# S4D convolution and spatial-shift mixer: the statistics of h for twelve token tiles move out of the convolution, two tiles of x are normalised on GpSimd, and the order of instructions is set anew

## The chip, the core and the metric

The kernel runs on one core of one Trainium2 chip. Its engines are TensorE (PE, matmuls; PEld is its loading of weights), VectorE (DVE), ScalarE (ACT), GpSimd (POOL) and SyncE (SP, which issues most transfers). Each engine works through its own instructions in their order and waits on semaphores for the others. The metric is the device time of one execution in microseconds; the median of several is given.

## What is computed

x is 2048 tokens by 512 channels. A layer norm of x goes through a long convolution whose kernel is made from complex poles (128 modes for each channel), with a skip term; x is added. The sum h is normalised and goes through a mixer: a layer, a shift of the tokens by one or two in four groups of channels, a second layer, then a two-layer MLP, with two further layer norms and residual sums.

```python
P = jnp.exp((A * dt[:, None])[:, :, None] * pos[None, None, :])
K = 2.0 * jnp.einsum("dn,dnl->dl", C, P).real
Kf = jnp.fft.rfft(K, L2)                      # L2 = 2 * 2048
Uf = jnp.fft.rfft(u_t, L2)
y = jnp.fft.irfft(Uf * Kf[None, :, :], L2)[:, :, :L]
...
h = x + _A_ref(_layernorm(x, axis=-1), ...)   # y + u * D_skip
h2 = h + _B_ref(_layernorm(h, axis=-1), B_w1, B_w2, B_w3, B_w4)
```

In `_B_ref`: `h = gelu(LN(x) @ w1)`, four channel groups shifted by +1, -1, +2 and -2 tokens, `x1 = x + hs @ w2`, `x1 + gelu(LN(x1) @ w3) @ w4`.

## The kernel before

`h` holds x, later h, as 128 partitions (tokens) by 16 token tiles j by 512 channels, for the whole run. The kernel has two phases.

**The convolution** (`conv_phase`, line 304) transforms tokens by a two-stage FFT of length 4096 written as matmuls. The channels go in four spans s of 128 (`WID`), each made of eight groups g of 16 channels (`CH`). For each group, `table(g)` (line 570) builds the powers of the poles: `phases` adds two integer parts on GpSimd into `pt`, ScalarE takes sine and cosine of `pt`, and products of `E` and `ec` give amplitudes, `amx` for one stage and `amp` for the other; products `cs<-pt,amx`, `cs<-pt,amp`, `sn<-pt,amp` are the tables. `taps` turns them into the convolution's kernel by matmuls, the first stage of its transform follows (`stage_a_taps`, where ScalarE copies banks of PSUM to `at`, or `stage_a_turn`, where VectorE transposes the bank and PE needs fewer matmuls). For the tokens, `stage_a_x` and `spectrum_x` do the same; the spectra of spans 3 and 2 (`FAR`) are made early and wait in DRAM.

Each span ends with eight steps e: `product(s, e)` (line 803) multiplies two spectra into `u`, on VectorE (`u<-xs,bank`, 128 x 1024) or on GpSimd; where the table `SHARE["sum" + s]` names e, two sums `u<-u` of 128 x 256 halve the matmuls of the following `stage_b_inv` (`u,ms`, 16 in place of 32). `stage_a_inv` and `last_a_inv` finish the inverse and add to h. While span 3 is finished, bn_stats over the 384 channels of the other spans runs on the sixteen tiles (line 1097); `finish(q)` adds the last 128 channels of tiles 4q to 4q+3 and aggregates, for q = 0 to 2 in the mixer.

**What sets the order.** `Plan` is a list scheduler: each node has an engine, an estimated cost, what it reads and writes, and may have a due time made from the table `NOM`. `SHARE` says for each kind of step which groups, for the even and the odd spans, run on which engine (`amy`: amp on GpSimd, the others on VectorE; `csy`, `sny`: cs and sn with amp on GpSimd; `sq`: squares of amx on ScalarE, the others by the wider 896-column VectorE form; `turn`, `hadd`, `mul0`, `sum0` ... as their names say). Where PE would be idle the plan puts matmuls on `ident` that produce nothing that is used. Every instruction is issued by one helper, so nearly all have the same line, 86.

**The mixer** (`mixer_phase`, line 1124) is written in program order. `norm1(q)` applies the norm to four tiles (`xl`), `turn1(q)` transposes them on PE (`transposed`, into banks `xt`) and `split` makes a high part on ScalarE (`xt30h`) and a low part on VectorE (`xt30l`); `layer1(q, f)` multiplies by w1 in three products (`PROD`). The link from the convolution:

```python
norm1(3), finish(0), turn1(3), gelus(), root([0]), norm1(0), finish(1)
layer1(3, 0), layer1(3, 1), finish(2), layer1(3, 2), turn1(0), root([1, 2]), layer1(3, 3), norm1(1), raw3(0), raw4(0)
```

`some(13)` (lines 1527 and 1534) issues thirteen queued steps of the second norm at a slice of layer 3.

Of the kernel before, what the change touches and what calls it, by code (L numbers as in the profile page):

```python
# [1586 lines left out]
```

## Time and profile before

| | us |
| --- | --- |
| median of 3 runs | 716.33 (716.03 to 716.98) |
| the profiled execution | 715.36 |
| its span in the trace | 713.5 |
| PE busy | 664.4, 93% of the span |
| VectorE busy | 539.1, 76% |
| ScalarE busy | 420.5, 59% |
| GpSimd busy | 378.9, 53% |

The span is what the trace covers of the profiled execution. The shares of busy time are averages over stages that differ: x is loaded up to about 28 us; tables, spectra and spans 0 to 2 follow to about 283; span 3's products and inverses (called the tail) run to about 306; the link to about 330; then the mixer. Rows of groups read: out<-in, partitions x elements, count | busy us, mean ns of one | idle time before them and what ended it. Rows of the chain and the timeline begin with the start and the duration in us; square brackets hold the engine's idle time before the row and what ended it.

### The profile page before, as it was taken

Reading aid. Unit: us, or ns where it says so; the run is one execution under the profiler, and the core shown is the slowest. Engines: PE = TensorE matmul, PEld = TensorE weight load, DVE = VectorE, ACT = ScalarE, POOL = GpSimd, SP = SyncE. Lnnn points to the kernel's source line nnn. Section 1 sums busy time; section 2 is a strip of 40 time slices with the busy share of each in tenths; the row PEclk is TensorE's granted clock in tenths of the full one; section 3 lists DMA queues with packets and bytes.
Section 4 is the critical chain, followed back from the end, with each engine's and each line's share of the span. In section 5 each row is a group of like instructions: output and inputs, shape, how many; then the busy total and the mean of one; then the engine's idle time right before and its main releaser. Section 6 shows DMA issues by size and latency. Waiting matters only on the chain.

```text
span 713.5 us, 17581 instructions
## 1 busy us (share of the span) xinstructions
PE 664.4 (93%) x7324; PEld 522.9 (73%) x7324; DVE 539.1 (76%) x931; ACT 420.5 (59%) x724; POOL 378.9 (53%) x371
## 2 busy tenths in 40 slices
PE   5893899799999898989999999999999999999997
PEld 5892566575575584848888877888888888888886
DVE  6999997999999999987464777945568955544544
ACT  7789679777797886237536345555535544444430
POOL 1785676859989995302445304655343655543310
PEclk9997899999999999999999999999999999999999
DMA  8830154211301123010011001211111252112014
GB/s 210 263 124 16 47 166 152 61 38 40 62 18 31 46 86 98 2 60 1 1 30 30 1 3 57 60 48 57 45 46 43 79 158 60 45 45 58 3 28 118
DMA packets 44915, 45.24 MB, mean 63 GB/s; under 512 B 4900, under 2 KB 31524, under 8 KB 44836
## 3 DMA queue, kind: packets, MB, share of 16 engines
q1 hardware_dynamic: 44068, 43.07, 21.3%
q10 hardware_dynamic: 768, 1.05, 0.6%
q8 instruction: 57, 0.93, 0.6%
q14 instruction: 22, 0.18, 0.1%
HBM read 35.72 MB, written 8.39 MB: 62 GB/s over the span
## 4 chain that ended last, share of the span: by engine, by line
PE 58%; DVE 17%; ACT 15%; issue 4%; DMA 3%; POOL 2%; SPq 1%; DVEq 0%; ACTq 0%; POOLq 0%
PE l L86 21%; PE acc L86 10%; PE bank L86 7%; ACT pt L86 7%; DVE u L86 5%; DMA h<-in_A_u_dram 3%; PE l3f L86 3%; PE l3a L86 3%; PE l3b L86 3%; PE l3e L86 3%; PE l3c L86 3%; PE l3d L86 2%; PE l3g L86 2%; DVE cs L86 2%; DVE sn L86 2%
## 5 line engine op out<-in xcount | busy, mean ns | idle before, releaser
L86 ACT ACTIVATE pt<-pt 128x1056 f32<-128x1056 int32 x64 | 70.0, 1094 | 9.7 <-DVE cs L86 7.1
L86 POOL TENSOR_TENSOR pt<-p,s 128x1024 int32<-128x1024 int32 x32 | 65.0, 2035 | 14.5 <-DVE sn L86 13.1
L86 PE MATMUL bank<-at,tbs 128*64 128x128 f32 (+1 forms) x768 | 63.5, 311 | 2.8 <-DVE u L86 1.1
L86 PEld LDWEIGHTS bank<-at,tbs 128*64 128x64 f32 x768 | 44.5, 134 | 18.2 <-DVE u L86 2.6
L86 PE MATMUL bank<-u,ms 64*128 64x128 f32 x768 | 51.8, 281 | 3.7 <-DVE u L86 1.8
L86 PEld LDWEIGHTS bank<-ident 128*128 128x128 f32 x396 | 48.8, 203 | 6.5 <-issue 1.9
L86 PE MATMUL bank<-ident 128*128 128x128 f32 x396 | 51.8, 291 | 1.1 <-ACT at L86 1.1
L86 PEld LDWEIGHTS bank<-u,ms 64*128 64x128 f32 x768 | 45.7, 187 | 9.4 <-DVE u L86 2.4
L86 PE MATMUL bank<-cs 128*32 128x64 f32 x1024 | 33.8, 227 | 16.5 <-DVE scratch L86 12.9
L86 ACT COPY at<-bank 128x512 f32<-128x512 f32 x48 | 30.1, 636 | 30.5 <-PE bank L86 30.4
L86 PEld LDWEIGHTS bank<-cs 128*32 128x32 f32 x1024 | 25.1, 113 | 29.7 <-issue 20.8
L86 DVE TENSOR_TENSOR cs<-pt,amx 128x512 f32<-128x512 f32 x64 | 41.2, 683 | 5.8 <-ACT pt L86 2.9
L86 POOL TENSOR_TENSOR cs0w<-raw,cs0w 128x512 fp32r<-128x512 f32 x7 | 9.1, 1296 | 67.5 <-ACT cs0w L86 58.8
L86 DVE TENSOR_TENSOR u<-u,l3f 128x512 f32<-128x512 f32 x14 | 9.6, 685 | 44.5 <-PE l3f L86 44.5
L86 DVE TENSOR_TENSOR h<-h,l 128x512 f32<-128x512 f32 x48 | 32.4, 686 | 13.4 <-PE l L86 13.3
L86 POOL TENSOR_TENSOR cs1w<-raw,cs1w 128x512 fp32r<-128x512 f32 x7 | 9.2, 1308 | 60.6 <-ACT cs1w L86 57.7
L86 ACT ACTIVATE pt<-pt,halfpi 128x1056 f32<-128x1056 f32 x32 | 38.1, 1190 | 0.5
L86 ACT ACTIVATE u<-u 128x512 f32<-128x512 f32 x56 | 35.4, 633 | 1.8
L86 PE MATMUL bank<-sn 128*32 128x64 f32 x1024 | 32.8, 225 | 1.5 <-DVE sn L86 1.5
L86 POOL TENSOR_TENSOR amp<-E,ec 128x512 f32<-128x512 f32 x28 | 31.0, 1112 | 4.6 <-DVE ec L86 4.2
L86 DVE STREAM_TRANSPOSE at<-bank 128x1024 f32<-128x1024 f32 (+1 forms) x32 | 30.0, 979 | 2.6 <-PE bank L86 2.6
L86 POOL TENSOR_TENSOR cs<-pt,amp 128x512 f32<-128x512 f32 x23 | 28.0, 1215 | 7.1 <-ACT pt L86 4.1
(1160 smaller groups left out, 2108.8 us busy)
## 6 DMA issues: line engine op xcount, KB each, us to landing
raw<-in_B_w_dram SPq DMA_DIRECT2D x28, 256.0 KB, 2.8
h<-in_A_u_dram SPq DMA_DIRECT2D x32, 128.0 KB, 4.3
h<-in_A_u_dram SPq DMA_DIRECT2D x16, 256.0 KB, 4.1
rawa<-in_B_w_dram SPq DMA_DIRECT2D x14, 256.0 KB, 2.9
rawb<-in_B_w_dram SPq DMA_DIRECT2D x14, 256.0 KB, 2.9
ms<-in_mm_dram SPq DMA_DIRECT2D x4, 768.0 KB, 11.6
out_dram<-h SPq DMA_DIRECT2D x48, 64.0 KB, 1.7
xs<-far SPq DMA_DIRECT2D x10, 256.0 KB, 2.9
```

Source lines behind the costliest of these rows:

```text
L86: ins = f(*args, **kw)
```

## The change

The statistics over 384 channels stay in the convolution for tiles 12 to 15 alone, each held back to one of the first four products of span 3 (`BS`). Tiles 0 to 11 get one bn_stats over all 512 channels in `finish`, in the mixer, in two halves placed apart in the link; `root([1, 2])` is split in two. `norm_x` takes a slightly shorter rsqrt and gives tiles 4 and 15 of x to GpSimd (`nrm`). `phases` becomes two nodes of 8 channels each over half the columns; the two sums of a product become two nodes. In the link, all banks of `transposed` are of the wide kind; for q = 3, tiles 12 and 13 are turned first, then c by c the other two, each c split at once; `layer1(3, 0)` takes products of high parts ahead of low ones. `some(13)` becomes `some(11)`. `SHARE` and `NOM` get new values, so the whole order of the convolution is set anew. By the counts of the two programs' instructions, VectorE gets 13 amp products (4 before), 19 amx products of 896 columns (14), 13 of 512 (18) and 24 transposes of a bank (16), and loses 12 of its 44 statistics, 5 of 16 cs and sn products with amp, 4 of 16 sums `u<-u`, 4 of 8 additions of h and one normalisation. GpSimd has 19 amp products (28), 28 sums (16), 53 cs and sn products (48), 64 half phases (32 whole). PE has 352 matmuls `u,ms` (384), 352 `fas`/`kt` ones (576) and 231 fillers (198).

```diff
@@ line 24 @@
-    'amy': [[0, 1, 3, 4, 5, 6, 7], [0, 1, 2, 3, 4, 5, 6]],
-    'turn': [[2, 4, 5, 7], [5]],
-    'sum3': [[0, 4, 5, 6, 7], [0, 2]],
+    'nrm': [[4], [7]],
+    'amy': [[0, 1, 3, 4, 5, 6, 7], [1, 2, 3, 6]],
+    'turn': [[1, 2, 3, 5, 6, 7], [0, 3, 4, 5, 6, 7]],
+    'sum3': [[0, 1, 3, 4, 5, 6, 7], [0, 1, 2, 7]],
...
+BS = (0, 1, 2, 3)
@@ line 584 before, 585 after @@
-        def phases():
-            n = 2 * CH
-            o, o8 = slice(g % PG * n, g % PG * n + n), slice(g % NT * n, g % NT * n + n)
+        def phases(i):
+            n = CH
+            o, o8 = (slice(k * 2 * n + i * n, k * 2 * n + i * n + n) for k in (g % PG, g % NT))
             gp.tensor_tensor(
-                pi.rearrange("p (d i) -> p d i", i=33)[:, :, 0:32].rearrange("p d (a b) -> p d a b", b=8),
+                pi.rearrange("p (d i) -> p d i", i=33)[:, i * n : i * n + n, 0:32].rearrange("p d (a b) -> p d a b", b=8),
                 p8[:, o, :].unsqueeze(2).to_broadcast([128, n, 4, 8]),
@@ line 600 before, 601 after @@
-        add("POOL", 1.91, phases, r=["p8", "s"] + (["p81", "s1"] if 0 < g < PG else []), w=[kp])
+        for i in range(2):
+            add("POOL", 0.99, lambda i=i: phases(i), r=["p8", "s"] + (["p81", "s1"] if 0 < g < PG else []), w=[kp])
         if g == 0:
@@ line 844 before, 846 after @@
             add("ACT", 0.22 + n * 0.51e-3, lambda: act.copy(tap, taps_()), w=[uk], frees=p)
-            add("POOL", 3.0, pooled, r=keys, w=[uk])
+            add("POOL", 3.0, pooled, r=keys, w=[uk, ("made", s, e)])
         else:
-            add("DVE", 0.07 + 2 * n * 1.06e-3, mult, r=keys, w=[uk], frees=p)
+            add("DVE", 0.07 + 2 * n * 1.06e-3, mult, r=keys, w=[uk, ("made", s, e)], frees=p)
         eng = "POOL" if e in SHARE[f"sum{s}"][1] else "DVE" if e in SHARE[f"sum{s}"][0] else None
...
-            def sums():
-                en.tensor_tensor(q[:, 0], q[:, 0], q[:, 3], ALU.subtract)
-                en.tensor_tensor(q[:, 1], q[:, 1], q[:, 2], ALU.add)
-            add(eng, 2 * dve(2 * w_) if eng == "DVE" else 1.3, sums, w=[uk], port=True)
+            c = dve(2 * w_) + 0.02 if eng == "DVE" else 0.65
+            add(eng, c, lambda: en.tensor_tensor(q[:, 0], q[:, 0], q[:, 3], ALU.subtract), w=[uk], port=True)
+            add(eng, c, lambda: en.tensor_tensor(q[:, 1], q[:, 1], q[:, 2], ALU.add), w=[uk], port=True)
@@ line 974 before, 974 after @@
-        rs, la, lb, nb = (bs[:, :, 1, i] for i in range(4))
+        rs, lb, nb = (bs[:, :, 1, i] for i in range(3))
         root = lambda: plan.view(first)[:, 0:16]
...
             lambda: v.tensor_scalar(root(), mv[:, :, 1], EPS, None, ALU.add),
-            lambda: v.tensor_scalar(la, mv[:, :, 1], EPS, None, ALU.add),
             lambda: v.tensor_scalar(root().bitcast(I32), root().bitcast(I32), 1, None, ALU.logical_shift_right),
...
             ops += [
-                lambda: v.tensor_tensor(lb, la, root(), ALU.mult),
+                lambda: v.scalar_tensor_tensor(lb, mv[:, :, 1], EPS, root(), ALU.add, ALU.mult),
                 lambda: v.scalar_tensor_tensor(lb, lb, -0.5, root(), ALU.mult, ALU.mult),
...
         for i, op in enumerate(ops):
-            n = add("DVE", 0.09, op, r=["mv"], w=["rs"], bank=i == 0, frees=first if i + 1 == len(ops) else None, port=i == 1)
+            n = add("DVE", 0.09, op, r=["mv"], w=["rs"], bank=i == 0, frees=first if i + 1 == len(ops) else None)
             first = n if i == 0 else first
...
         for j in R16:
-            if j < LND:
+            if j % 8 in SHARE["nrm"][j // 8]:
+                add("POOL", 1.2, lambda j=j: gp.tensor_scalar(
+                    h[:, j, :], h[:, j, :], mv[:, j, 0:1], rs[:, j : j + 1], ALU.subtract, ALU.mult),
+                    r=["mv", "rs"], w=[("x", j // 2, c) for c in R4])
+            elif j < LND:
                 add("DVE", 0.46, lambda j=j: v.tensor_scalar(
@@ line 1094 before, 1097 after @@
         else:
-            for j in R16:
+            for i, j in enumerate(range(12, 16)):
                 add("DVE", 0.48, lambda j=j: v.bn_stats(bs[:, j, 0, :], h[:, j, 0 : OFF[s]]),
-                    r=[("h", q, r) for q in range(s) for r in range(WID[q] // 32)], w=[("bs", j)],
+                    r=[("h", q, r) for q in range(s) for r in range(WID[q] // 32)] + [("made", s, BS[i])], w=[("bs", j)],
                     at=TS[s] + NOM["st"] + 2 * j)
...
-    def finish(q):
-        for j in range(4 * q, 4 * q + 4):
+    def finish(q, tiles=range(4)):
+        for j in (4 * q + i for i in tiles):
             if q < 3:
-                v.bn_stats(bs[:, j, 1, :], h[:, j, OFF[NS - 1] :])
-        for j in range(4 * q, 4 * q + 4):
-            v.bn_aggr(cst["mv"][:, j, :], bs[:, j].rearrange("p a b -> p (a b)"))
+                v.bn_stats(bs[:, j, 0, :], h[:, j, :])
+        for j in (4 * q + i for i in tiles):
+            v.bn_aggr(cst["mv"][:, j, :], bs[:, j, 0, :] if q < 3 else bs[:, j].rearrange("p a b -> p (a b)"))
@@ line 1177 before, 1181 after @@
-    def transposed(tiles, name, wide=True, cs=range(4)):
-        b = [wide_bank(c, f"{name}_{c}") if wide else bank(f"{name}_{c}") for c in cs]
-        turn = lambda i, c: nc.tensor.transpose(b[c][:, i * 128 : i * 128 + 128], tiles[i][:, c * 128 : c * 128 + 128], ident)
-        if wide:
-            return [[turn(i, c) for i in range(4)] and split(b[c], f"{name}{c}") for c in cs]
-        for i in range(4):
-            for c in cs:
+    def transposed(tiles, name, first=0):
+        b = [wide_bank(c, f"{name}_{c}") for c in range(4)]
+        def turn(i, c):
+            nc.tensor.transpose(b[c][:, i * 128 : i * 128 + 128], tiles[i][:, c * 128 : c * 128 + 128], ident)
+        for i in range(first):
+            for c in range(4):
                 turn(i, c)
-        return [split(b[c], f"{name}{c}") for c in cs]
+        res = []
+        for c in range(4):
+            for i in range(first, 4):
+                turn(i, c)
+            res.append(split(b[c], f"{name}{c}"))
+        return res
@@ line 1205 before, 1216 after @@
     def turn1(q):
-        XT[q] = transposed(XL.pop(q), f"xt{q}", q < 3)
+        XT[q] = transposed(XL.pop(q), f"xt{q}", 2 if q == 3 else 0)
...
         n = 0
-        for c in range(4):
-            for wi, xi in (PROD if q < 3 else PROD[::2] + PROD[1:2]):
-                nc.tensor.matmul(b, W1[f][wi][:, c * 128 : c * 128 + 128], XT[q][c][xi],
-                                 start=(n == 0), stop=(n == 11))
-                n += 1
+        seq = [(c, wi, xi) for c in range(4) for wi, xi in PROD]
+        if (q, f) == (3, 0):
+            seq.sort(key=lambda k: 2 * k[0] + 3 * k[2])
+        for c, wi, xi in seq:
+            nc.tensor.matmul(b, W1[f][wi][:, c * 128 : c * 128 + 128], XT[q][c][xi], start=(n == 0), stop=(n == 11))
+            n += 1
         H1[q, f] = gelu(b, f"h1_{q}_{f}")
@@ line 1381 before, 1394 after @@
     gelus = lambda: nc.scalar.activation(zero, zero, AF.Gelu_apprx_tanh)
-    norm1(3), finish(0), turn1(3), gelus(), root([0]), norm1(0), finish(1)
-    layer1(3, 0), layer1(3, 1), finish(2), layer1(3, 2), turn1(0), root([1, 2]), layer1(3, 3), norm1(1), raw3(0), raw4(0)
-    layer1(0, 0), layer1(0, 1), layer1(0, 2), turn1(1), layer1(0, 3), layer2(0), layer2(1)
+    early, late = range(2), range(2, 4)
+    norm1(3), finish(0, early), turn1(3), gelus(), finish(0, late), root([0]), norm1(0)
+    layer1(3, 0), layer1(3, 1), finish(1, early), layer1(3, 2), turn1(0), finish(1, late), root([1]), layer1(3, 3), norm1(1), raw3(0), raw4(0)
+    layer1(0, 0), layer1(0, 1), finish(2, early), layer1(0, 2), finish(2, late), layer1(0, 3), turn1(1), root([2]), layer2(0), layer2(1)
     norm1(2), sum3(), layer1(1, 0), layer1(1, 1), layer1(1, 2), turn1(2), layer1(1, 3), load3(0), raw3(1)
@@ line 1517 before, 1531 after @@
                 stats2(j)
-            todo.extend(norm2_ops(2)), some(13)
+            todo.extend(norm2_ops(2)), some(11)
         if s == 2:
...
                 stats2(j)
-            todo.extend(norm2_ops(3)), some(13)
+            todo.extend(norm2_ops(3)), some(11)
         if s == 3 or s == 4:
```

How it moves instructions, at three places (names end in a buffer's number).

VectorE in the tail (`u0` and `u1` are the two buffers of products, `bs` the statistics). Before, from ahead of the third product of span 3:

```order
L86 BN_STATS bs_65<-h_63 128x6 x4
L86 TENSOR_TENSOR u1_121<-scratch_103,bank2_83 128x1024
L86 BN_STATS bs_65<-h_63 128x6 x2
L86 TENSOR_TENSOR u0_120<-scratch_103,bank3_84 128x1024
L86 BN_STATS bs_65<-h_63 128x6 x4
L86 TENSOR_TENSOR u1_121<-scratch_103,bank2_83 128x1024
L86 TENSOR_TENSOR u1_121<-u1_121 128x256 x2
L86 TENSOR_TENSOR u0_120<-scratch_103,bank3_84 128x1024
L86 TENSOR_TENSOR u0_120<-u0_120 128x256 x2
L86 BN_STATS bs_65<-h_63 128x6
L86 TENSOR_TENSOR u1_121<-p8_108,bank2_83 128x1024
```

After, from behind the first product:

```order
L87 BN_STATS bs_65<-h_63 128x6
L87 TENSOR_TENSOR u1_121<-xs1_123,bank0_81 128x1024
L87 BN_STATS bs_65<-h_63 128x6
L87 TENSOR_TENSOR u0_120<-scratch_103,bank2_83 128x1024
L87 BN_STATS bs_65<-h_63 128x6
L87 TENSOR_TENSOR u1_121<-scratch_103,bank3_84 128x1024
L87 BN_STATS bs_65<-h_63 128x6
L87 TENSOR_TENSOR u1_121<-u1_121 128x256 x2
L87 TENSOR_TENSOR u0_120<-scratch_103,bank2_83 128x1024
L87 TENSOR_TENSOR u0_120<-u0_120 128x256 x2
L87 TENSOR_TENSOR u1_121<-scratch_103,bank3_84 128x1024
```

The groups of two and four statistics between the products are gone, and single ones stand behind each of the first four. The fourth product (the second into `u1` of those shown after) now has its two sums ahead of the fifth.

PE in the link, from the turn of tile 14 to the first bank of layer 1 (`xt3_c` are the banks of the turned tiles 12 to 15, `xt3ch` and `xt3cl` their high and low parts, `cs0w` and `cs1w` hold parts of the first weights). Before:

```order
L86 MATMUL xt3_0_4161<-ident_58,xl14_4149 128x128
L86 MATMUL xt3_1_4162<-ident_58,xl14_4149 128x128
L86 MATMUL xt3_2_4163<-ident_58,xl14_4149 128x128
L86 MATMUL xt3_3_4164<-ident_58,xl14_4149 128x128
L86 MATMUL xt3_0_4161<-ident_58,xl15_4151 128x128
L86 MATMUL xt3_1_4162<-ident_58,xl15_4151 128x128
L86 MATMUL xt3_2_4163<-ident_58,xl15_4151 128x128
L86 MATMUL xt3_3_4164<-ident_58,xl15_4151 128x128
L86 MATMUL l1_3_0_4226<-xt30h_4181,cs0w_3727 128x512 x2
L86 MATMUL l1_3_0_4226<-xt30l_4182,cs0w_3727 128x512
L86 MATMUL l1_3_0_4226<-xt31h_4185,cs0w_3727 128x512 x2
L86 MATMUL l1_3_0_4226<-xt31l_4186,cs0w_3727 128x512
```

After:

```order
L87 MATMUL xt3_0_3952<-ident_58,xl14_3944 128x128
L87 MATMUL xt3_0_3952<-ident_58,xl15_3946 128x128
L87 MATMUL xt3_1_3953<-ident_58,xl14_3944 128x128
L87 MATMUL xt3_1_3953<-ident_58,xl15_3946 128x128
L87 MATMUL xt3_2_3954<-ident_58,xl14_3944 128x128
L87 MATMUL xt3_2_3954<-ident_58,xl15_3946 128x128
L87 MATMUL xt3_3_3955<-ident_58,xl14_3944 128x128
L87 MATMUL xt3_3_3955<-ident_58,xl15_3946 128x128
L87 MATMUL l1_3_0_4013<-xt30h_3966,cs0w_3536 128x512 x2
L87 MATMUL l1_3_0_4013<-xt31h_3972,cs0w_3536 128x512 x2
L87 MATMUL l1_3_0_4013<-xt30l_3967,cs0w_3536 128x512
L87 MATMUL l1_3_0_4013<-xt32h_3978,cs0w_3536 128x512 x2
```

The last two tiles are turned c by c, and each low part is used one step later, behind the next c's high part.

GpSimd at the end of the tables, around the last phases (`pt<-p8,s8`). Before:

```order
L86 TENSOR_TENSOR pt_112<-p8_108,s8_109 128x32x32
L86 TENSOR_TENSOR cs1_115<-pt_112,amp0_118 128x512
L86 TENSOR_TENSOR sn1_117<-pt_112,amp0_118 128x512
L86 TENSOR_TENSOR u0_120<-u0_120 128x256 x2
L86 TENSOR_TENSOR pt_112<-p8_108,s8_109 128x32x32
L86 TENSOR_TENSOR amp0_118<-E1_105,ec_102 128x512
L86 TENSOR_TENSOR sn0_116<-pt_112,amp0_118 128x512
L86 TENSOR_TENSOR u0_120<-u0_120 128x256 x2
L86 TENSOR_TENSOR cs1_115<-pt_112,amp0_118 128x512
```

After:

```order
L87 TENSOR_TENSOR pt_112<-p8_108,s8_109 128x16x32 x2
L87 TENSOR_TENSOR u0_120<-u0_120 128x256 x2
L87 TENSOR_TENSOR cs1_115<-pt_112,amp0_118 128x512
L87 TENSOR_TENSOR sn1_117<-pt_112,amp0_118 128x512
L87 TENSOR_TENSOR u1_121<-u1_121 128x256
L87 TENSOR_TENSOR pt_112<-p8_108,s8_109 128x16x32
L87 TENSOR_TENSOR u1_121<-u1_121 128x256
L87 TENSOR_TENSOR pt_112<-p8_108,s8_109 128x16x32
L87 TENSOR_TENSOR sn0_116<-pt_112,amp0_118 128x512
```

Each phase is in two halves, and single sums of a product stand between them.

More of the change, by code (lines that the diff above doesn't have):

```diff
@@ L23 @@
 PG = 4
-SHARE = {'mul0': [[1, 4], [0]], 'mul2': [[], []], 'amy': [[0, 1, 3, 4, 5, 6, 7], [0, 1, 2, 3, 4, 5, 6]], 'csy': [[5, 7], [0, 1, 2, 3, 4, 5, 7]], 'sny': [[1, 2, 6, 7], [0, 1, 2, 4, 5, 6, 7]], 'sq': [[0, 1, 2, 3, 5, 7], [1, 2, 4, 6]], 'turn': [[2, 4, 5, 7], [5]], 'hadd': [[0, 2, 6], [2, 3, 4, 5]], 'sum0': [[1, 2, 4], [4]], 'sum1': [[2], [5, 6]], 'sum2': [[4, 6, 7], [2, 4, 6]], 'sum3': [[0, 4, 5, 6, 7], [0, 2]]}
+SHARE = {'nrm': [[4], [7]], 'mul0': [[], [7]], 'mul2': [[6], []], 'amy': [[0, 1, 3, 4, 5, 6, 7], [1, 2, 3, 6]], 'csy': [[1, 4, 5, 6, 7], [0, 1, 2, 3, 4, 5, 7]], 'sny': [[1, 2, 3, 5, 6, 7], [0, 1, 2, 4, 5, 6, 7]], 'sq': [[0, 1, 5, 7], [1, 4, 7]], 'turn': [[1, 2, 3, 5, 6, 7], [0, 3, 4, 5, 6, 7]], 'hadd': [[0, 1, 2, 4, 6], [0, 2, 3, 5]], 'sum0': [[1, 4, 5], [1, 3, 4, 6]], 'sum1': [[0, 1], [0, 1]], 'sum2': [[1, 3], [1, 4, 5, 6]], 'sum3': [[0, 1, 3, 4, 5, 6, 7], [0, 1, 2, 7]]}
 XS = 2
@@ L34 @@
 LOOK = 0.05
+BS = (0, 1, 2, 3)
 FILL0 = 8.0
 FILLC, FILLN = 0.3, 128
-NOM = {'t0': 5334.34, 'per': 269.07, 'ln': 726.1, 'kg0': -4330.77, 'kgs0': -265.35, 'kg': 1.37, 'kgs': 337.02, 'ak': 482.29, 'ax': -575.41, 'b': -3.66, 'ib': -188.65, 'y': 2171.48, 'ys': 152.77, 'tr': 2105.83, 'exp': 1024.14, 'wt': 5260.29, 'pr1': 2915.83, 'pr2': 5242.12, 'st': -122.8, 'xa': -796.93, 'xs': -1631.75}
+NOM = {'t0': 7043.75, 'per': -130.02, 'ln': 950.41, 'kg0': -4725.44, 'kgs0': 3.78, 'kg': -162.35, 'kgs': 340.97, 'ak': 3031.32, 'ax': -642.19, 'b': 80.14, 'ib': -31.03, 'y': 3997.86, 'ys': 390.75, 'tr': 2244.98, 'exp': 3135.42, 'wt': 8336.6, 'pr1': 3284.83, 'pr2': 6195.32, 'st': -1499.02, 'xa': 896.41, 'xs': -2350.92}
 TURN = 2.0 ** 32
```

## The prediction

> **What bounds the kernel.** I read the busy shares by stage first, then the chain of waits, then the groups of the stage that the change rewrites. The windows (microseconds from the span's start) show four regimes:
>
> ```profile
> core 0: us, PE busy (x) PEld busy (x) DVE busy (x) ACT busy (x) POOL busy (x), PEclk, DMA share, GB/s
> 28.00:275.00 247.00, 215.59 (x4871) 157.30 (x4870) 230.54 (x349) 198.19 (x342) 195.24 (x169) 0.96 0.26 78
> 283.40:305.70 22.30, 22.10 (x309) 18.37 (x310) 21.96 (x37) 6.68 (x11) 6.67 (x8) 1.00 0.05 14
> 305.00:420.00 115.00, 111.64 (x546) 88.81 (x546) 75.58 (x185) 57.67 (x102) 36.34 (x62) 1.00 0.06 19
> 420.00:713.50 293.50, 288.49 (x1276) 236.32 (x1274) 183.96 (x288) 132.01 (x221) 124.47 (x110) 1.00 0.21 58
> ```
>
> From 28 to 275 (the body: tables, spectra, three spans) DVE is busy 230.54 of 247, ahead of every other engine: DVE sets the body. From 283.4 to 305.7 (the tail: the last span's products and inverses) PE and DVE are both full. From 305 on (link and mixer) PE is, and DVE has room. The chain of waits, in order of time, names the same:
>
> ```profile
> 283.38 13.66 PE bank L86 x199
> ...
> 299.14 0.47 DVE bs L86
> ...
> 303.91 1.85 DVE bs L86 x4
> ```
>
> So the tail runs along PE, with a stray statistic of h (`bs`) of 0.47 on the path.
>
> **Body, DVE: +6.2 us by rows.** Groups of DVE in the body (out<-in, shape, count | busy us, mean ns | idle before):
>
> ```profile
> L86 DVE TENSOR_TENSOR u<-xs,bank 128x1024 f32<-128x1024 f32 x21 | 25.5, 1217 | 2.4 <-ACT xs L86 2.2
> L86 DVE TENSOR_TENSOR amx<-E,amx 128x896 f32<-128x896 f32 x14 | 15.3, 1089 | 2.5 <-ACT amx L86 2.2
> L86 DVE TENSOR_TENSOR amx<-E,amx 128x512 f32<-128x512 f32 x17 | 11.7, 691 | 0.4 <-ACT amx L86 0.4
> L86 DVE STREAM_TRANSPOSE at<-bank 128x512 f32<-128x512 f32 x12 | 7.8, 696 | 0.0
> L86 DVE TENSOR_TENSOR u<-u 128x256 f32<-128x256 f32 x8 | 7.6, 991 | 0.0
> L86 DVE TENSOR_TENSOR cs<-pt,amp 128x512 f32<-128x512 f32 x9 | 6.5, 718 | 0.0
> L86 DVE TENSOR_TENSOR amp<-E,ec 128x512 f32<-128x512 f32 x4 | 3.2, 795 | 0.0
> ```
>
> Counting the instructions of the two programs, DVE gains nine amp products (9 x 0.795 = 7.2), eight transposes of a bank (8 x 0.696 = 5.6), five amx products in the 896 form (5 x 1.089 = 5.4) and one product of a spectrum (1.2): 19.4. It loses five amx products in the 512 form (3.5), five table products with amp (5 x 0.718 = 3.6), two additions of h and one normalisation of x (3 x 0.7, by the rows of the same size), and four sums u<-u (4 x 0.991 = 4.0): 13.2. Net +6.2. Nothing covers this, since the stage is DVE's.
>
> What gives some back. First, DVE's own waits in the body (instruction, releaser: us, count, longest):
>
> ```profile
> DVE cs L86 <- ACT pt L86: 2.9, 2, 2.0
> DVE amx L86 <- ACT amx L86: 2.6, 5, 1.0
> DVE cs L86 <- ACT amx L86: 2.2, 3, 0.9
> ```
>
> ACT squares amx for 13 groups instead of 18 and copies eight banks fewer, which DVE now transposes. The waits on squares fall by 5/18 of 4.8 (1.3); of the 2.9 on a late pt I take 1.2: -2.5, with 0 and -7.7 as ends. Second, waits that DVE spends inside an instruction beside GpSimd. The same u<-u takes 0.422 in the tail, where GpSimd is nearly idle, and one DVE step took 2.04 us beside a phase product:
>
> ```profile
> L86 DVE TENSOR_TENSOR u<-u 128x256 f32<-128x256 f32 x8 | 3.0, 422 | 0.1
> 132.46 2.04 DVE L86 SCALAR_TENSOR_TENSOR scratch<-scratch 128x256 f32<-128x256 f32 x1
> 132.27 1.95 POOL L86 TENSOR_TENSOR pt<-p,s 128x1024 int32<-128x1024 int32 x1
> L86 DVE TENSOR_TENSOR amp<-E,ec x4: 680/702/1095, 32.4 to 270.6; 128x512 f32<-128x512 f32 x4
> ```
>
> The two ran together and ended together, 134.50 and 134.22. The eight sums lost 8 x (0.991 - 0.422) = 4.6 that way. With each phase product cut into two halves of half the length, I take half of that, -2.3; the ends are +4.6 (other steps are caught as often, in place of those removed) and -4.6. Body: 6.2 - 2.5 - 2.3 = +1.4, between about +11 and -6.
>
> Here a rule of the Trainium skill speaks against the change: "SBUF — State Buffer", section "Who interferes with whom", says that VectorE and GpSimd share one port pair as an exclusive lock, that a VectorE instruction with two SBUF inputs contends with a GpSimd one that reads SBUF, and that whoever issues second is blocked for the whole instruction. The row at 132.46 agrees. By that rule the nine amp products (E and ec both in SBUF) would each wait about half a GpSimd operation, 0.6, and the body would be about 5 dearer (an estimate by that page). The amp row (shortest, median, longest) has a median of 0.702 and a longest of 1.095, so three in four were hardly held up, and I do not add it.
>
> **Body, GpSimd: about +2 us, hidden.**
>
> ```profile
> L86 POOL TENSOR_TENSOR pt<-p,s 128x1024 int32<-128x1024 int32 x30 | 61.1, 2040 | 14.4 <-DVE sn L86 13.1 <-DVE bs L86 0.9
> L86 POOL TENSOR_TENSOR amp<-E,ec 128x512 f32<-128x512 f32 x28 | 31.0, 1112 | 4.6 <-DVE ec L86 4.2
> L86 POOL TENSOR_TENSOR cs<-pt,amp 128x512 f32<-128x512 f32 x23 | 28.0, 1215 | 7.1 <-ACT pt L86 4.1 <-PE bank L86 1.8 <-issue 1.2
> L86 POOL TENSOR_TENSOR u<-u 128x256 f32<-128x256 f32 x12 | 8.9, 766 | 3.4 <-DVE u L86 3.2
> ```
>
> Nine amp products leave (-10.0), five cs/sn come (+6.1), eight sums come in the body (+6.1), two u<-u,xs products go (-2.6 at 1.3 each). Two normalisations of x come: no GpSimd row has one; between 0.77 and 2.04 each, nearest the 512-wide rows, 1.2 each (+2.4). The 32 added starts of half phases lie within these. Net +2 on 195.24 of 247: covered by 50 us of slack; were it gone, the pt of the next group would be late and DVE's waits on pt grow.
>
> PE needs 215.59 of 247 there; its 32 fewer matmuls of u, and the fas,kt shift to the turned form, cost nothing, since DVE hides it. SP's queue has the same 213 issues, a few swapped.
>
> **Tail: -2.0 us.** DVE drops twelve of sixteen 384-wide statistics, all eight products are summed instead of six, and GpSimd sums the last one too:
>
> ```profile
> L86 DVE BATCH_NORM_STATS2 bs<-h 128x6 f32<-128x384 f32 x16 | 7.9, 548 | 0.0
> 286.65 2.06 PE L86 MATMUL bank<-u,ms 64*128 64x128 f32 x32
> 289.67 1.16 PE L86 MATMUL bank<-u,ms 64*128 64x128 f32 x16
> 293.27 1.43 POOL L86 TENSOR_TENSOR u<-u 128x256 f32<-128x256 f32 x2 [1.30 <-DVE u L86]
> ```
>
> Two inverses shrink from 32 to 16 matmuls (2 x 0.90 = -1.8), and statistics of 0.47 leave the path between products in two places (-0.9). The last product's pair of sums goes to GpSimd, 1.43 instead of 2 x 0.422 on DVE, and only the last inverse can follow it: +0.7 (rounded up for the hand-over). The same on products 0 to 2 lies beside the next product. The block of four statistics at 303.91 filled DVE's wait for the last inverse and gives nothing. One end is -8: all that DVE drops (12 x 0.548 = 6.6, two additions of h 1.4), as if DVE alone set it. The other is 0: the short inverses only let PE fill the time with idle matmuls. I take -2.0, since PE is at 22.10 of 22.30, so the relief of the chain counts and not DVE's total.
>
> **Link: -0.9 us.** The new order has transposes of the last tiles ready c by c, high products ahead of low ones, and no bank shared with the split:
>
> ```profile
> 316.05 1.94 PE L86 MATMUL xt<-ident,xl 128*128 128x128 f32 x16 [0.95 <-ACT h L86]
> 319.12 0.73 PE L86 MATMUL l<-xt30h,cs0w 128*128 128x512 f32 x2 [1.13 <-DVE xt30l L86]
> 323.06 1.52 ACT L86 ACTIVATE xl<-h,rn,rr 128x512 f32<-128x512 f32 x2 [1.73 <-DVE rn L86]
> 327.42 1.91 PE L86 MATMUL xt<-ident,xl 128*128 128x128 f32 x16
> L86 DVE BATCH_NORM_STATS2 bs<-h 128x6 f32<-128x128 f32 x12 | 2.6, 278 | 0.0
> L86 DVE BATCH_NORM_STATS2 bs<-h 128x6 f32<-128x512 f32 x16 | 10.5, 670 | 0.9 <-DMA h<-in_A_u_dram 0.9
> ```
>
> PE's 1.13 wait on the split xt30l falls by about half (-0.6); the first c is complete after 10 of 16 transposes rather than 13, 0.12 each (-0.3). DVE's statistics grow from 0.278 to 0.670 on twelve tiles (+4.7) and the split roots add eleven small steps (at most +4.6, at 0.422, the shortest DVE row shown): all behind PE, which has 111.64 of 115 while DVE has 75.58. What is queued behind them on DVE is rn for tiles 0 to 3, so xl starts later by 4 x 0.39 - 0.3 = 1.3: from 323.06 plus two activations to 327.42, where PE turns them, there are some 2.8 us, less the 0.9 that PE arrives earlier. That margin of 0.6 keeps it covered; without it, up to 1 us returns.
>
> **Mixer: -0.5 us.** Two fewer queued steps are issued ahead of a slice's gelus in two places:
>
> ```profile
> 441.01 1.52 ACT L86 ACTIVATE x<-x,qo,qr 128x512 f32<-128x512 f32 x2 [4.97 <-DVE qo L86]
> 445.10 0.50 PE L86 MATMUL l<-cs0w,h_001h 128*128 128x512 f32 x1 [0.53 <-DVE u L86]
> ```
>
> PE's 0.53 at 445.10 goes, since the two activations of 1.52 no longer precede the gelu it needs. Ends 0 and -1.
>
> **Sum.** +1.4 - 2.0 - 0.9 - 0.5 = -2.0 on the profiled execution's 715.36, so 713.4; that execution stands 0.97 below the runs' median of 716.33, so I forecast a median of 714.3. A measurement of this kernel can tell about 0.2% from no change, 1.4 us.
>
> **Rivals.** (1) No change that can be told: the body costs about as much as the other stages save, +3.4 against -3.4: 716.3. For it: DVE's work over body and tail together stays nearly equal (+6.2 against -8), so the order mostly moves it to where DVE is also the limit. (2) The tail gets 6 of the 8 that DVE drops, and the body recovers all 6.2 from the waits above: -7.4 with link and mixer, 708.9. For it: DVE is at 21.96 of 22.30 in the tail; against: so is PE. (3) Slower: DVE's extra work in the body is paid in full, because the steps held up beside GpSimd are now the amp products and transposes in place of the sums, and half phases catch DVE twice as often for half as long. Place: the body; price +6.2, against -2.0 and -1.4: +2.8, 719.1. From a body of +4.8 on, that is with less than 1.4 of the 6.2 recovered, the kernel is measurably slower. For it: the amp product of 1.095 and the scratch step of 2.04; against: the median of 0.702. The rule of the Trainium skill named above stands beside this rival.
>
> **Numbers.** Chances: forecast 0.42, (1) 0.16, (2) 0.18, (3) 0.24. Faster by over 0.2%: 0.34 of the forecast and all of (2), 0.52. Within 0.2%: 0.08 of the forecast and all of (1), 0.24. Slower: 0.24. The range takes in the rivals' times with half a microsecond beyond, 708.5 to 719.5, and leaves out the far ends of the body (+11, -6); the forecast's own is 712.0 to 716.0.
>
> **What would show it.** In the profile after: u<-u on DVE in the body nearer 0.6 than 0.99 (phases halved), amp on DVE near 0.70 over thirteen of them, the start of the tail's first product within 2 us of 283, the tail about 20 long, no statistic of h of 384 columns outside tiles 12 to 15, layer 1's first product waiting under 0.6, and xt of tiles 0 to 3 not waiting on ACT. I am wrong if the tail starts 4 us or more later, if amp on DVE averages over 1 us, or if PE waits on xl.

## The result and the profile after

| | before | after |
| --- | --- | --- |
| median, us | 716.65 (716.03 to 717.20, 6 runs) | 709.89 (709.72 to 712.03, 6 runs) |
| profiled execution, us | 715.36 | 709.74 |
| its span, us | 713.5 | 707.6 |

The ratio of the two means is 0.9914, with a 95% interval of 0.9899 to 0.9928: 6.2 us faster, between 5.2 and 7.2 (the medians lie 6.8 apart). The forecast was 714.3, 2.0 us faster, in a range from 708.5 to 719.5.

Where the time came from is read best from a few events that both kernels have (start in us, in the profiled executions):

| event | before | after | earlier by |
| --- | --- | --- | --- |
| first product of span 3 (VectorE), end of the body | 284.99 | 280.05 | 4.94 |
| first transpose of the last inverse, end of the tail | 305.68 | 300.69 | 4.99 |
| first product of layer 1, link | 319.12 | 313.16 | 5.96 |
| transposes for the second norm's first tiles | 376.58 | 371.28 | 5.30 |
| layer 3 behind the slice with the queued steps | 448.15 | 442.01 | 6.14 |
| last 24 matmuls | 703.83 | 697.62 | 6.21 |

Nearly all of it is the body, the stage for which the prediction added time. The tail gave nothing, the link 1.0 and the mixer 0.8, of which 0.7 were lost between.

The body in both kernels, from 28 us to the first product of span 3; first before, then after:

```profile
28.00:284.98 256.98, 223.99 (x5067) 160.85 (x5066) 239.88 (x361) 202.65 (x349) 201.53 (x173) 0.96 0.27 80
```

```profile
28.00:280.04 252.04, 231.12 (x4659) 162.68 (x4661) 237.31 (x365) 199.54 (x337) 214.05 (x209) 0.98 0.27 80
```

The columns are the stretch, its length, and the busy time of PE, PEld, VectorE, ScalarE and GpSimd, each with its instructions. VectorE is 239.88 busy, then 237.31, with four instructions more. So VectorE did the longer list of work in less busy time, and its idle time fell from 17.1 to 14.7 us. GpSimd got 12.5 us more work and carried it. The groups that changed, of before (this stage; rows that stand in the prediction are not shown again):

```profile
L86 DVE TENSOR_TENSOR scratch<-scratch 128x256 f32<-128x256 f32 x5 | 6.5, 1315 | 0.0
L86 DVE SCALAR_TENSOR_TENSOR scratch<-scratch 128x256 f32<-128x256 f32 x7 | 4.8, 690 | 0.1
L86 DVE TENSOR_SCALAR sh<-thp 128x256 int32<-128x256 int32 x6 | 4.1, 676 | 0.0
L86 DVE TENSOR_TENSOR sn<-pt,amp 128x512 f32<-128x512 f32 x7 | 4.9, 695 | 0.0
```

And of after:

```profile
L87 DVE TENSOR_TENSOR cs<-pt,amx 128x512 f32<-128x512 f32 x64 | 41.3, 682 | 3.2 <-ACT pt L87 2.1 <-ACT amx L87 0.6
L87 DVE TENSOR_TENSOR amp<-E,ec 128x512 f32<-128x512 f32 x13 | 11.2, 869 | 0.0
L87 DVE TENSOR_TENSOR cs<-pt,amp 128x512 f32<-128x512 f32 x6 | 6.3, 1052 | 0.0
L87 DVE TENSOR_TENSOR sn<-pt,amp 128x512 f32<-128x512 f32 x5 | 5.4, 1080 | 0.0
L87 DVE TENSOR_TENSOR scratch<-scratch 128x256 f32<-128x256 f32 x5 | 4.5, 929 | 0.0
L87 DVE SCALAR_TENSOR_TENSOR scratch<-scratch 128x256 f32<-128x256 f32 x7 | 2.8, 413 | 0.0
L87 DVE TENSOR_TENSOR u<-u 128x256 f32<-128x256 f32 x4 | 2.0, 511 | 0.0
L87 DVE TENSOR_SCALAR sh<-thp 128x256 int32<-128x256 int32 x6 | 1.7, 290 | 0.0
```

The same `scratch` and `sh` steps, small ones that prepare a group of channels, cost 15.4 us before and 9.0 after (6.5 + 4.8 + 4.1 against 4.5 + 2.8 + 1.7), and a sum `u<-u` 0.511 instead of 0.991. The products with amp are longer than before (1.052 and 1.080 against 0.718 and 0.695). So the time that VectorE spends held up inside its instructions has moved to other steps and shrunk, by more than the prediction allowed. Its sum can be estimated: group VectorE's instructions in the body by operation, names and shape, and add up what each takes above the shortest of its group in the profiles of four kernels. That gives 34.2 us before and 25.7 after; of two kernels that come below, `b_half` has 32.9 and `a_whole` 29.2.

### The profile page after: what moved, and what is told of

Its sections match the earlier page's. It is cut to its first block, busy times and chain, and to the rows that moved or that the text cites. A ratio compares the mean times of both kernels' runs of the same rounds, so it can differ in the third digit from the quotient of the medians.

```text
span 707.6 us, 16728 instructions
## 1 busy us (share of the span) xinstructions
PE 671.8 (95%) x6886; PEld 524.0 (74%) x6886; DVE 538.2 (76%) x933; ACT 415.6 (59%) x708; POOL 393.2 (56%) x411
## 3 DMA queue, kind: packets, MB, share of 16 engines
q10 hardware_dynamic: 768, 1.05, 0.7%
## 4 chain that ended last, share of the span: by engine, by line
PE 56%; DVE 22%; ACT 8%; POOL 5%; issue 4%; DMA 3%; SPq 1%; DVEq 0%; POOLq 0%; ACTq 0%
PE l L87 18%; PE acc L87 11%; PE bank L87 8%; ACT pt L87 4%; DVE u L87 4%; DVE at L87 3%; DVE cs L87 3%; PE l3c L87 3%; PE l3f L87 3%; PE l3e L87 3%; DVE sn L87 3%; PE l3a L87 3%; PE l3d L87 3%; PE l3b L87 3%; PE l3g L87 3%
## 5 line engine op out<-in xcount | busy, mean ns | idle before, releaser
L87 ACT ACTIVATE pt<-pt 128x1056 f32<-128x1056 int32 x64 | 69.8, 1091 | 14.6 <-POOL pt L87 7.2
L87 POOL TENSOR_TENSOR pt<-p,s 128x512 int32<-128x512 int32 x64 | 70.9, 1122 | 6.0 <-DVE sn L87 5.6
L87 PEld LDWEIGHTS bank<-ident 128*128 128x128 f32 x462 | 59.1, 208 | 7.1 <-issue 4.6
L87 PE MATMUL bank<-ident 128*128 128x128 f32 x462 | 63.9, 297 | 0.0
L87 PE MATMUL bank<-u,ms 64*128 64x128 f32 x704 | 48.2, 282 | 3.2 <-DVE u L87 2.2
L87 PEld LDWEIGHTS bank<-u,ms 64*128 64x128 f32 x704 | 42.2, 187 | 8.5 <-issue 2.2
L87 DVE TENSOR_TENSOR h<-h,l 128x512 f32<-128x512 f32 x48 | 32.6, 687 | 14.8 <-PE l L87 14.7
L87 ACT COPY at<-bank 128x512 f32<-128x512 f32 x40 | 25.0, 626 | 28.7 <-PE bank L87 28.7
L87 DVE STREAM_TRANSPOSE at<-bank 128x512 f32<-128x512 f32 (+1 forms) x40 | 35.4, 925 | 2.7 <-PE bank L87 2.7
L87 POOL TENSOR_TENSOR cs<-pt,amp 128x512 f32<-128x512 f32 x26 | 32.8, 1262 | 5.9 <-DVE amp L87 3.5
L87 POOL TENSOR_TENSOR sn<-pt,amp 128x512 f32<-128x512 f32 x27 | 33.4, 1238 | 2.1 <-ACT pt L87 1.2
```

What stands on the lines that cost most here:

```text
L87: ins = f(*args, **kw)
```

## The experiments

Each run is compared with runs of the kernel before on its own chip; the ratio is that of the two. A remark for reading the profiles: three kernels whose order of the body is that of the kernel after (this kernel, `a_sum7`, `a_sumVh`) had their first product of span 3 at 280.05, 279.11 and 277.64, and four with that of before (that kernel, `b_link`, `b_some11`, `b_tail8`) at 284.99, 283.91, 285.50 and 285.23. Two executions of one body so differ by up to 2.4 us. About 1.2 of this lies ahead of the body: VectorE's first `cs<-pt,amx` starts at 27.75, 26.50 and 26.54, and at 28.19, 27.39, 28.20 and 27.31. From that product on, the means are 252.0 and 257.1, so the body is 5.1 shorter by all seven profiles, and 4.5 by the two kernels' own.

**Halves and tables: is it the half phases, or the new order?** Four kernels. `b_half` is the kernel before with

```diff
         def phases():
-            n = 2 * CH
-            o, o8 = slice(g % PG * n, g % PG * n + n), slice(g % NT * n, g % NT * n + n)
+            n = CH
+            for i in range(2):
+                o, o8 = (slice(k * 2 * n + i * n, k * 2 * n + i * n + n) for k in (g % PG, g % NT))
...
```

> The kernel before with each phase product on GpSimd issued as two halves of eight channels, back to back at the same place; nothing else changes. In the kernel after, VectorE's small steps and products in the body lose some 12 us less beside GpSimd, and the body is 4.9 us shorter. Theory A (short holds: half phases hold VectorE up half as long): the body gets 3 to 5 us shorter, about 712.5 us, and scratch, sh and u<-u on VectorE get shorter, as in the kernel after. Theory B (it is the new order that keeps these steps away from GpSimd): no change, 716.2 to 717.4, since the order is that of before. Theory C (halves cost GpSimd more than they give, 0.1 us a phase by the two means, 2.04 and 2 x 1.12): 717.5 to 719.

Measured: 1.0001 (0.9989 to 1.0013) of the kernel before, no change.

`a_whole` is the kernel after with the first half's step issuing the whole phase, and the second's nothing:

```diff
         def phases(i):
+            if i:
+                return
+            n = 2 * CH
```

> The kernel after with each phase product whole, issued where the first half stood; the order is otherwise the same. Theory A: 3 to 5 us slower than the kernel after, 713 to 715. Theory B: within 0.8 us of it, 709.1 to 710.7. Theory C: somewhat faster than the kernel after, 708 to 709.5.

Measured: 0.9997 (0.9985 to 1.0009) of the kernel before, against 0.9914 with halves: 0.83% or 5.9 us of 716 slower than the kernel after, nearly all of the 6.2 that it had gained.

`b_tables` is the kernel before with the two lines `SHARE` and `NOM` of after, `a_oldtab` the reverse:

```diff
-SHARE = {...}    # one kernel's own
-NOM = {...}
+SHARE = {...}    # the other's
+NOM = {...}
```

> The kernel before with the shares and due times of the kernel after (without the two normalisations on GpSimd): whole phases, sixteen statistics in the conv, the old link. Theory A: little gain or a loss in the body, 715 to 719, since the shares add work to VectorE and the holds stay long. Theory B: most of the body's gain, 711 to 713. The old link and the thirteen steps keep 1.3 us of the difference in both.

> The kernel after with the shares and due times of the kernel before: half phases, statistics in the mixer, new link, eleven steps. Theory A: 710 to 712.5 (the halves' gain and 1.3 us of link and mixer; the tail keeps its two long inverses). Theory B: 714.5 to 716 (link and mixer alone).

Measured: 1.0186 (1.0170 to 1.0202) and 1.0179 (1.0157 to 1.0200), both slower than every theory had it.

None of the theories stands as it was put. Halves alone give nothing, the tables alone cost 13 us, the rest of the code without them 13 us as well; only the kernel with both gains. Most of the loss in the two crossed kernels is waiting on VectorE. From 28 to 290 us, ahead of the first product of span 3 in both, first `b_tables`, then `a_oldtab`:

```profile
28.00:290.00 262.00, 235.96 (x4670) 163.63 (x4669) 235.15 (x363) 195.58 (x331) 200.23 (x174) 0.97 0.25 76
28.00:290.00 262.00, 222.94 (x5044) 163.43 (x5053) 236.32 (x353) 201.68 (x348) 202.15 (x200) 0.96 0.24 74
```

VectorE is idle for 26.9 and 25.7 us, against 17.1 and 14.7 in the bodies of before and after. In `b_tables` the tail is longer too (26.96 instead of 20.69).

What the halves do in each order is seen on the steps that GpSimd can hold up. GpSimd and VectorE in `b_half`, body:

```profile
L86 POOL TENSOR_TENSOR pt<-p,s 128x512 int32<-128x512 int32 x60 | 69.3, 1179 | 7.8 <-DVE sn L86 5.3 <-ACT pt L86 1.0 <-DVE bs L86 0.6
L86 DVE TENSOR_TENSOR u<-u 128x256 f32<-128x256 f32 x8 | 6.1, 798 | 0.0
L86 DVE TENSOR_TENSOR scratch<-scratch 128x256 f32<-128x256 f32 x5 | 4.8, 978 | 0.0
28.00:285.59 257.59, 224.14 (x5073) 160.97 (x5071) 238.53 (x360) 203.53 (x350) 208.71 (x204) 0.97 0.27 78
```

VectorE's held-up steps did get shorter (its busy time fell from 239.88 to 238.53 in a body 0.6 longer), but a pair of halves costs GpSimd 2.31 (69.3 / 30) instead of 2.04, 8.2 us over the body, and VectorE waited 2.0 more for others: 19.1 us idle instead of 17.1. In `a_whole`, where only the length of the phase differs from the kernel after:

```profile
28.00:284.15 256.15, 228.85 (x4642) 160.60 (x4641) 241.54 (x366) 200.12 (x339) 207.35 (x179) 0.98 0.26 79
L87 DVE TENSOR_TENSOR cs<-pt,amp 128x512 f32<-128x512 f32 x6 | 7.7, 1288 | 0.0
L87 DVE TENSOR_TENSOR u<-u 128x256 f32<-128x256 f32 x4 | 3.1, 766 | 0.0
```

Here busy time is 4.2 above that of the kernel after (241.54 against 237.31) and idle time the same (14.6 against 14.7), and the body is 4.1 longer. In the new order the halves are worth their whole saving of held-up time; in the old one it turns into waits. By the sums of held-up time given above, the new order alone took 5.0 off (34.2 to 29.2), the halves another 3.5 (to 25.7). Whether an order found for whole phases would do as well stays open, since that was not tried.

**Nine amp products, in both orders.** In `b_amp` and `a_amp` the nine products go to the other engine, each at its place in the order that is kept. The two lists of `amy` stand for the first span (g below 8) and for the three others, not for even and odd spans, so the three entries that the second list loses are nine products:

```diff
-        add(e, c, lambda: outer(eng, amy, ...), ...)
+        real = gp if g % 8 in OTHER[g >= 8] else v    # OTHER: the list 'amy' of the other kernel
+        add(e, c, lambda: outer(real, amy, ...), ...)
```

> The kernel before with the nine amp products that the change takes from GpSimd issued on VectorE, each at its old place in the order. By the prediction's first line (rows: VectorE sets the body, 9 x 0.795): the body 7 us longer, 723 to 724. If an order leaves VectorE room beside such steps, or GpSimd's relief shortens its waits and holds as much as the nine cost: 715 to 718 on the same scale. If holds come on top (half a GpSimd operation each): 727 and more.

> The kernel after with the nine moved amp products back on GpSimd, each at its place in the new order. If VectorE's sum of work set the body, it would lose 9 x 0.87 = 7.8 us and the run be 4 to 8 us faster (in the old order the same nine cost 4.0 us on VectorE). If the new order lives on GpSimd being relieved, GpSimd (214 of 252 us busy, +10) is late with cs and sn and the run is 3 us or more slower than the kernel after. In between, 0 to 2 us either way: the engines balance.

Measured: `b_amp` 1.0058 (1.0044 to 1.0072), 4.2 us slower than before; `a_amp` 0.9974 (0.9965 to 0.9983), 0.60% or 4.3 us slower than the kernel after. The body windows of `b_amp` and of `a_amp`:

```profile
28.00:288.94 260.94, 224.04 (x5064) 160.76 (x5065) 245.66 (x370) 202.64 (x349) 193.10 (x164) 0.97 0.26 78
```

```profile
28.00:283.84 255.84, 229.83 (x4652) 160.19 (x4654) 233.15 (x354) 198.80 (x335) 220.69 (x218) 0.98 0.27 79
```

In the old order nine products add 5.8 to VectorE's busy time and 4.0 to the body, about half of the 7.2 that the rows give: the nine take 7.3 (0.811 each, the mean of all thirteen), the other steps together take 1.5 less, and idle time shrinks by 1.8. In the new order taking them off VectorE saves 4.2 of busy time and brings 8.0 of idle time (22.7 against 14.7). VectorE is the busiest engine there, and still its sum of work does not set the body: relieved, it waits for others. What grew most are its waits for the squares of `amx` on ScalarE (2.9 to 7.1 us) and for `xs` (0.6 to 2.5); why these came later was not followed.

**The normalisation of two tiles.** `a_nrmV` issues them on VectorE at the same place (`gp.tensor_scalar` becomes `v.tensor_scalar`).

> The kernel after with the two normalisations of x that GpSimd makes issued on VectorE at the same place of the order. GpSimd took 2.1 us for each and VectorE (1.1 us) and PE (1.3 us) waited for them once. If GpSimd's slowness there costs time: 0.5 to 1.5 us faster than the kernel after. If VectorE's time is what counts (two steps of 0.78): up to 1.5 us slower. If the place has slack: no change.

Measured: 0.9944 (0.9931 to 0.9958), 0.30% or 2.1 us slower than the kernel after, a difference known to about 1.4. On GpSimd (kernel after, body) each took 2.085, far above the 1.2 of the prediction:

```profile
L87 POOL TENSOR_SCALAR h<-h,mvh,bs 128x512 f32<-128x512 f32 x2 | 4.2, 2085 | 0.0
```

It is still the right engine: two steps off VectorE are worth about 2 us, 1.6 of it their own 0.794 each.

**Link, statistics and the mixer alone.** `b_link` is the kernel before with the statistics of tiles 0 to 11 in the mixer and the new link, so with the hunks on `finish`, `transposed`, `layer1` and the three lines of the link; `b_some11` has `some(11)` alone.

> The kernel before with the statistics of h for tiles 0 to 11 made in the mixer alone and with the new link (transposes, order of layer 1's first bank, roots apart); shares, due times and the order of the conv up to the tail are those of before. By the steps of the prediction: tail -0.9 (statistics off the path; the two long inverses stay), link -0.9: 1.8 us faster, a ratio near 0.9975. By what the profile of the kernel after suggests (tail unchanged at 20.6, layer 1 starts 1.0 earlier but 0.6 is given back behind the larger statistics): 0.4 to 0.7 us faster, ratio 0.999 to 0.9995.

> The kernel before with eleven queued steps of the second norm at the two slices in place of thirteen; nothing else. By the prediction: 0.5 us faster (the wait of PE at 445.10). By the profile after: 0.9 us faster (PE stands 5.27 earlier ahead of that place and 6.14 behind it).

Measured: `b_link` 0.9985 (0.9976 to 0.9994), 1.1 us faster, and `b_some11` 0.9991 (0.9980 to 1.0001), which leans to 0.6 faster but takes in no change. In `b_link` the tail (first product to first transpose) is 20.03 instead of 20.69: by the profiles the statistics are worth 0.7, not 0.9. The link (first transpose to layer 1's first product) takes 12.39 instead of 13.44: 1.05. PE in the link of the kernel after:

```profile
311.14 1.95 PE L87 MATMUL xt<-ident,xl 128*128 128x128 f32 x16 [1.01 <-ACT h L87]
313.16 0.74 PE L87 MATMUL l<-xt30h,cs0w 128*128 128x512 f32 x2
321.57 1.91 PE L87 MATMUL xt<-ident,xl 128*128 128x128 f32 x16
```

The wait of 1.13 on the low part is gone, and tiles 0 to 3 (321.57) wait for nothing.

**The tail: where the short inverses went.** `b_tail8` is `b_link` with all eight products of span 3 summed; `a_sum7` takes the last pair of sums off GpSimd; `a_sumVh` takes all four pairs off it and keeps PE's order.

```diff
# b_tail8
-'sum3': [[0, 4, 5, 6, 7], [0, 2]]
+'sum3': [[0, 1, 3, 4, 5, 6, 7], [0, 2]]
# a_sum7
-'sum3': [[0, 1, 3, 4, 5, 6, 7], [0, 1, 2, 7]]
+'sum3': [[0, 1, 3, 4, 5, 6, 7], [0, 1, 2]]
# a_sumVh
-            en = gp if eng == "POOL" else v
+            en = gp if eng == "POOL" and s < 3 else v
```

> b_link (statistics out of the tail, new link, order of before) with the products e = 1 and 3 of span 3 summed on VectorE too, so that all eight inverses are of 16 matmuls. By the prediction's term for the inverses (2 x 0.90 on PE's path): the tail 18.2 instead of the 20.03 of b_link, the run 1.8 us faster than b_link. If another chain than PE's matmuls sets the tail (product, sum, inverse, with idle matmuls filling PE): the tail 19.5 to 20.1 and the run within 0.5 us of b_link.

> The kernel after with the sums of the last product of span 3 on VectorE in place of GpSimd; no other instruction moves. By the prediction's term of +0.7 for that step: 0.6 to 0.7 us faster than the kernel after, and the tail 20.0 instead of 20.64 (last product to first transpose 3.8 instead of 4.4). If the last inverse waits for something else: no change.

> The kernel after with the sums of span 3's products 0, 1, 2 and 7 on VectorE in place of GpSimd, PE's order and its idle matmuls unchanged. If GpSimd's slow pairs ate the gain of the short inverses: product 2 no longer waits (1.5 us of waits on POOL u in the tail), the tail 18.5 to 19.3 instead of 20.64, the run 1.3 to 2 us faster than the kernel after. If only the last pair counts: 0.7 us faster, tail 19.9. It is also the candidate for a version faster than both.

Measured: `b_tail8` 1.0015 (1.0007 to 1.0024), 0.30% or 2.1 us slower than `b_link`, with a tail of 21.41 instead of 20.03. `a_sum7` 0.9916 (0.9900 to 0.9931), no difference from the kernel after that the interval can tell, with a tail of 19.92 instead of 20.64 in its profile. `a_sumVh` 0.9929 (0.9912 to 0.9947), also no better, tail 20.62. So the expected gain from short inverses is not there at all, and in the old order it is a loss of 2.1 us, 1.4 of it in the tail. PE in the tail of `b_tail8`:

```profile
285.83 1.10 PE L86 MATMUL bank<-at,tbs 128*64 128x128 f32 x16
286.87 0.94 PE L86 MATMUL bank<-ident 128*128 128x128 f32 x6
287.96 1.27 PE L86 MATMUL bank<-u,ms 64*128 64x128 f32 x16 [0.16 <-DVE u L86]
289.17 1.10 PE L86 MATMUL bank<-at,tbs 128*64 128x128 f32 x16
290.20 1.38 PE L86 MATMUL bank<-ident 128*128 128x128 f32 x10
291.51 1.16 PE L86 MATMUL bank<-u,ms 64*128 64x128 f32 x16
```

Where an inverse took 2.06, there are now idle matmuls (`ident`, 0.94 and 1.38) and an inverse of 1.16 to 1.27: PE would wait for the sums, the plan fills the wait, and the chain from product to sum to inverse sets the pace. The ten cost time themselves: GpSimd's sums for the second of these inverses ended at 290.88, and it began at 291.51. PE's 22.10 of 22.30 in the prediction was a bound for the old tail, with 1.9 of idle matmuls in it; it did not say what would be the bound once PE's work shrank.

In the kernel after, VectorE's products wait for GpSimd's sums in two places:

```profile
285.14 1.22 DVE L87 TENSOR_TENSOR u<-scratch,bank 128x1024 f32<-128x1024 f32 x1 [0.97 <-POOL u L87]
287.32 1.22 DVE L87 TENSOR_TENSOR u<-scratch,bank 128x1024 f32<-128x1024 f32 x1 [0.49 <-POOL u L87]
```

`a_sumVh` has neither wait, but there VectorE makes these sums itself and is busy for 17.7 of the 18.3 us from its first product to its last sum, so hardly any time is left to gain there. Its last sums (first row) end at 295.92, but PE's inverse starts at 296.42:

```profile
295.16 0.76 DVE L87 TENSOR_TENSOR u<-u 128x256 f32<-128x256 f32 x2
294.88 1.60 PE L87 MATMUL bank<-ident 128*128 128x128 f32 x12
296.42 1.16 PE L87 MATMUL bank<-u,ms 64*128 64x128 f32 x16
```

The twelve idle matmuls were put there for a slow pair on GpSimd and now hold the inverse up themselves. In `a_sum7`, where the plan put six instead (so more changed there than the one pair), the last inverse came 0.7 sooner after the first product.

## Why the prediction was right or wrong, point by point

- **Direction and range:** right, faster by a measurable amount, 709.9 within 708.5 to 719.5, and far outside the forecast's own 712.0 to 716.0. For the forecast the direction was luck: the gain came in the stage for which it had a cost, and the tail, where it had half of the gain, gave none. The time is nearly that of rival (2), 708.9, with half of its mechanism: the body recovered all that the rows added and more, the tail got none of what VectorE dropped. Of the signs, short sums (0.511), a first product of layer 1 without a wait, and `xt` of tiles 0 to 3 without one came true; `amp` near 0.70 (0.869) and a tail that starts within 2 us of 283 (280.05) did not.
- **Body, +1.4: the step that failed.** Measured 4.9 shorter in the two profiles (4.5 to 5.1 without what lies ahead of the body), so 6 us off. The count of instructions behind +6.2 was right, but it priced them by means of the old order, which hold the time spent held up, and it took the hold of all other steps as given. VectorE's busy time fell by 2.6 instead of rising by 6.2. Of these 8.8, the `scratch` and `sh` steps gave 6.4, which the prediction left at nothing, other small steps about 4, and the four remaining sums 1.9 (4 x 0.48); longer products with `amp` took 3.9 back (6 x 0.33 and 5 x 0.39), the `amp` products themselves 0.9; and two additions of h (1.3) that the prediction took out of the tail came out here. The term of -2.3 was half the hold of eight sums, four of which had been taken off with theirs already (4 x 0.991), so for the other four it stands for all of it. And a product added to VectorE costs the body about half of its own time, 4.0 for nine (`b_amp`), not all.
- **Body, VectorE's waits, -2.5:** right in size (17.1 to 14.7), not in its parts. The waits for squares fell by 2.9 and those for `pt` by 0.7, and two new ones of 1.1 came, one of them for a normalisation on GpSimd.
- **The halves as the cause of the relief:** half right. They are worth 4 us (profiles) to 6 us (runs) in the new order and nothing in the old (`a_whole`, `b_half`), so the price of -2.3 was neither. The larger part of the saved hold came with the new order.
- **GpSimd +2, hidden:** its busy time rose by 12.5 (201.53 to 214.05), 5.5 of it because a pair of halves costs 0.2 more than a whole phase (66.6 us for thirty pairs, 2.22, against 2.04) and 1.8 because a normalisation takes 2.085 instead of 1.2. Hidden it was, but for the one wait of 1.1.
- **Tail, -2.0:** measured 0. By the profiles, statistics -0.7 (said -0.9), the last pair on GpSimd +0.7 (said +0.7, `a_sum7`, though the time of its runs does not show it), which leaves 0 for the inverses (said -1.8): the end of 0 that the prediction named, with idle matmuls.
- **Link, -0.9:** 1.0 at layer 1's first product, 0.3 net at the second norm. The prediction had VectorE's statistics all behind PE. In the kernel before the chain runs along PE from 319.12 on; in the kernel after it runs along VectorE and ScalarE until 341.47, where a pair of statistics holds the low part of a layer 1 output. PE's matmuls there start 0.50 and 0.34 apart instead of 0.23, so about 0.4 of the 0.7 that was lost again is at this place:

```profile
339.42 1.20 DVE bs L87 x2
341.47 11.65 PE l L87 x50
```

- **Mixer, -0.5:** 0.84 by the events, 0.6 by `b_some11` with no change inside its interval.
- **The rule of the Trainium skill** ("SBUF — State Buffer", "Who interferes with whom"): its mechanism bears out, its use as a price against the change did not. By shortest, median and longest, two kinds of product on VectorE in `a_whole`, the second operand in PSUM (amx) or in SBUF (amp):

```profile
L87 DVE TENSOR_TENSOR cs<-pt,amx x64: 649/680/694, 28.2 to 272.3; 128x512 f32<-128x512 f32 x64
L87 DVE TENSOR_TENSOR cs<-pt,amp x6: 677/1200/2262, 30.6 to 264.6; 128x512 f32<-128x512 f32 x6
```

  The one never waits in 64 times, the other up to 1.6 us, less than one whole phase of 1.96. That agrees with the page, by which a VectorE instruction with two SBUF inputs contends with GpSimd's reads and one with a single SBUF input, outside the two-port modes, does not. The count of operands is not the whole of it here: `sh<-thp` reads one operand, and took 0.286 to 1.679 us in the kernel before, the longest beside a whole phase; in which mode it ran no run shows. The thirteen amp products cost 0.869 on the mean in the kernel after, 0.17 above the median of 0.702 by which the prediction set the rule aside (its sum took 0.795), where the estimate by that page added 0.6: which of them are caught is a matter of the order.

## What to carry to other kernels

A row's mean duration belongs to the order that it was measured in: where two engines hold each other up, price a moved step by its shortest duration and a range for the hold, and expect a new order to move the hold as much as the work. The busiest engine of a stage need not be its bound while it still waits 6% of the time; take some work off it in place and see whether the stage moves, before a sum over its rows is believed. And a stage that a plan fills with idle matmuls shows a full TensorE whatever bounds it: take them out of the count, and look for them when a wait that they were made for is gone.

## What the runs showed that was not expected

- A table of shares and due times belongs to the code that it was found for: crossed, each cost 1.8 to 1.9% (1.0186 and 1.0179), more than twice what the change gains.
- The longest hold seen on these steps is about as long as one GpSimd instruction: the longest less the shortest of a row is 1.76 for the sums of the kernel before (beside a whole phase of 2.00) and 1.10 for products of the kernel after (beside the end of another step and a half phase of 1.09):

```profile
L86 DVE TENSOR_TENSOR u<-u x8: 418/866/2178, 138.0 to 265.2; 128x256 f32<-128x256 f32 x8
```

```profile
L87 DVE TENSOR_TENSOR sn<-pt,amp x5: 684/695/1784, 30.7 to 242.0; 128x512 f32<-128x512 f32 x5
```

- GpSimd normalises a tile of 128 x 512 in 2.085 us, 2.6 times VectorE's 0.794, and slower than a product of two tensors of that size (1.16 to 1.26).
- Idle matmuls that keep TensorE occupied are in its queue like any others: twelve of them held a ready inverse up for half a microsecond.
